# A retention layer and a multiplicative feed-forward on one core: every engine's queue in a new order, with casts, copies and sums shared anew

## The chip, the cores and the metric

The kernel runs on one core of a Trainium2 chip. The metric is the device time of one execution in microseconds (us); lower is better. Four compute engines take part: TensorE (PE, with its weight loads shown as PEld), VectorE (DVE), ScalarE (ACT) and GpSimd (POOL). SyncE (SP) issues all the DMAs, loads, stores and DMA transposes, through one queue.

## The reference

Four batches of eight heads run a linear recurrence with a decay of their own per head over 768 tokens; its output, with the heads side by side, passes through a feed-forward with two multiplied branches and two more matrices.

```python
gamma = 1.0 - 2.0 ** (-5.0 - np.arange(H))          # B, H, S, D = 4, 8, 768, 64
for t in range(S):
    state = gamma * state + k[:, :, t] (outer) v[:, :, t]
    y[:, :, t] = scale * (q[:, :, t] @ state)
x = y.transpose(0, 2, 1, 3).reshape(3072, 512)
h = (x @ w1) * (x @ w2)                              # w1, w2: 512 x 1024
out = (h @ w3) @ w_out                               # w3: 1024 x 1024, w_out: 1024 x 512
```

## The kernel before

**Tiling.** The 3072 tokens are cut into twelve chunks `n` of 256, three per batch. Matrix work is in fp16 with sums in fp32. `w3 @ w_out` is multiplied once, ahead of the tokens, into eight blocks `W3O`: `cast_w3` makes fp16 of a loaded block of w3, `turn_w3` transposes it on PE, `turned_w3` copies it out of PSUM, `w3_mm` multiplies it with a cast block of w_out, `w3_out` stores the sum in SBUF.

**A chunk.** `cast` and `cast_v` make fp16 of q, k and v; v is multiplied by a decay on the way, in `cast_v`. q and k are transposed, by PE for chunks 0 to 4 (`turn`, `turned`), and by a DMA for chunks 5 to 11 (`dma_turn`). `scores` multiplies k with q, `mask` takes the causal part out of PSUM, `kv` makes the state's increment, `state` adds it up, `inter` applies the state, `av` the masked scores. `x_out` takes x out of PSUM and multiplies it by the decay of q (table `YS` or `YN`).

**The feed-forward.** Chunks 0 and 1 multiply `W1` and `W2` in the plain way, one block of rows at a time as the weights arrive (`rows`, `rows_out`). From chunk 2 on, the two products are made by seven block products in place of eight: `combine` makes sums of weight blocks once (`WT`), `sums` makes sums of x blocks per chunk, `prod(n, u, i)` is one product (eight matmuls of 128 columns) for half `u` of the columns, `seed` and `keep_part` copy running sums out of PSUM, `c12` and `c22` add them, `half_h` multiplies the two branches. `o_unit` multiplies by `W3O`, `o_copy` scales the result into SBUF, `o_store` and `o_store_all` send it to HBM.

**Order.** Nothing is scheduled by a program: each engine executes its instructions in the order of the calls. In this text stage `n` is what stands between `inter(n, 0)` and `inter(n+1, 0)`. For n = 3 to 11 the order is a loop, whose PE part is: `inter(n,0)`, `kv(n+1)` and `scores(n+1)`, `inter(n,1)`, `av(n)`, two `o_unit(n-1, .)`, and fourteen `prod(n, ., .)`. SP too is one queue: a `dma_turn` that waits for its `cast` holds up the loads behind it. Loads go into 18 buffers (`NSTAGE`) of one pool `st`; the four `WT` tiles, and the output tiles of chunks 5 to 11, take buffers of the same pool. `fetch` is a load in the part before the loop.

Of the kernel before, what the change touches and what calls it, by code (L numbers as in the profile page):

```python
# [21 lines left out]
def kernel(  # L22
# [16 lines left out]
    NSTAGE = 18  # L39
# [138 lines left out]
    VN = const.tile([128, 2, H], FP, name="VN")  # L178
    YS = const.tile([128, 2, NP, 128], FP, name="YS")
# [10 lines left out]
    W3O = [wpool.tile([128, DM], HP, name=f"w3o_{i}") for i in range(8)]  # L190
# [179 lines left out]
    def scores(n, tags, hp=None):  # L370
# [10 lines left out]
        else:  # L381
            ps = [bank(t, [128, NP, 2, 64]) for t in tags]
            for a in range(NP):
                for s in range(2):
                    for r, g in QUARTERS:
                        nc.tensor.matmul(
                            ps[r][half(g), a, s, :], lhsT=kT[n][half(r), s, a, half(g)],
                            rhs=qchunk(n, r, a, s, g), start=True, stop=True,
# [144 lines left out]
    def x_out(n, g):  # L533
# [5 lines left out]
        if n < EO:  # L539
# [4 lines left out]
            )  # L544
        else:
# [73 lines left out]
    def o_unit(n, tb, tags, cuts=((0, 512),)):  # L619
        assert ht_n[n] == 4  # L620
        for (c0, c1), tag in zip(cuts, tags):
# [3 lines left out]
            for f in range(8):  # L625
                for x in range(parts):
                    nc.tensor.matmul(  # L627
                        ps[:, x * w : (x + 1) * w], lhsT=HT[n][:, tb, f, :], rhs=W3O[f][:, c0 + x * w : c0 + (x + 1) * w],
# [4 lines left out]
    def o_part(n, tb, x, tag):  # L633
# [4 lines left out]
        for f in range(4 * x, 4 * x + 4):  # L638
            nc.tensor.matmul(  # L639
                ps[:, :], lhsT=HT[n][:, tb, f, :], rhs=W3O[f][:, :], start=(f == 0), stop=(f == 7),  # L640
            )
# [15 lines left out]
    def o_copy(n, tb, c0=0, c1=512):  # L657
        nc.scalar.activation(o_tile(n, tb)[:, c0:c1], o_ps.pop((n, tb, c0, c1))[:, :], AF.Copy, scale=final_scale)  # L658
        o_n[n] = o_n.get(n, 0) + (c1 - c0)
        o_n[n, tb] = o_n.get((n, tb), 0) + (c1 - c0)  # L660

# [170 lines left out]
    fetch("r1")  # L832
    fetch("r5")
    fetch("r4")
    fetch("wo0")
    fetch("r2")
    fetch("wo2")
    fetch("r3")
    fetch("wo1")
    fetch("r6")  # L840
    fetch("k0")
    fetch("r7")
    fetch("wo3")
# [12 lines left out]
    fetch("w20")
    fetch("w23")
    fetch("k2")
    fetch("q2")
    fetch("q4")  # L860
    fetch("v2")
    fetch("q3")
    fetch("k3")
    fetch("v3")
    late_numbers()
    cast_w3_half(1, 0, "g")
    cast_w3_half(1, 1, "v")
    numbers()
    identity()
    keeps()  # L870
    cast_w3_half(4, 1, "g")
    cast_w3(2, "g")
    warm(2, "F2")
    warm(8, "X1")
    warm(3, "F2")
    turn_w3_half(1, 0, "F0")
    warm(3, "F2")
    turn_w3_half(1, 1, "S0")
    turn_w3_half(4, 1, "S0")
# [72 lines left out]
    w3_out(6, "s")
    cast_w3(0, "g")
    step_decays()
    w3_out(3, "v")
    mask(0, 0, 0)
    mask(0, 1, 0)
    state(0, 1)
    mask(0, 0, 1)
    w3_out(7, "s")  # L960
    state(0, 2)
    mask(0, 1, 1)
    inter(0, 0, ("F0", "X1"))
    turn("q", 1, "F1")
    turn_w3(0, "S0")
    fence(0)
    state(0, 3)
    turned_w3(0, "v")
    inter(0, 1)
    av(0)  # L970
    cast("k", 1, "s")
    turned("q", 1, "v")
    cast_wh(W1, "w1", 1, 0, "s")
    turn("k", 1, "X0")
    cast_v(1, "g")
    turned("k", 1, "v")
    x_out(0, 0)
    x_out(0, 1)
    w3_mm(0, 0)
    w3_mm(0, 2)  # L980
    scores(1, ("S0", "X0"), 1)
    w3_mm(0, 3)
    cast_wh(W1, "w1", 1, 1, "g")
    mask(1, 1, 1)
    w3_mm(0, 1)
    scores(1, ("F0", "K"), 0)
    kv(1, ("S1", "X1"))
    rows(W1, 0, 0, 1)
    cast_wc(W1, "w1", 0, 0, "g")
    cast_wh(W1, "w1", 3, 0, "g")  # L990
    cast_wc(W1, "w1", 2, 1, "g")
    cast_wc(W1, "w1", 2, 0, "g")
    w3_out(0, "s")
    cast_wc(W1, "w1", 0, 1, "s")
    cast_wh(W1, "w1", 3, 1, "s")
    mask(1, 1, 0)
    mask(1, 0, 1)
    state(1, 1)
    rows(W1, 0, 0, 0)
    rows(W1, 0, 1, 0)  # L1000
    rows(W1, 0, 1, 1)
    inter(1, 0, ("S0", "S1"))
    rows(W1, 0, 1, 3)
    rows(W1, 0, 0, 3)
    rows(W1, 0, 1, 2)
    fence(1)
    mask(1, 0, 0)
    state(1, 2)
    rows_out("a", 0, 1, 0, "s")
    cast_wh(W2, "w2", 1, 0, "v")  # L1010
    cast_wh(W2, "w2", 1, 1, "v")
    cast_wc(W2, "w2", 2, 1, "g")
    inter(1, 1)
    av(1)
    rows(W1, 0, 0, 2)
    rows_out("a", 0, 1, 1, "v")
    rows_out("a", 0, 0, 1, "s")
    cast_wc(W2, "w2", 2, 0, "s")
    cast_wh(W2, "w2", 3, 1, "s")
    x_out(1, 0)  # L1020
    rows(W2, 0, 1, 2)
    rows(W2, 0, 1, 1)
    rows(W2, 0, 0, 1)
    rows_out("a", 0, 0, 0, "v")
# [36 lines left out]
    rows(W2, 1, 0, 3)
    rows(W2, 1, 0, 0)
    rows(W2, 1, 1, 2)
    rows(W2, 1, 1, 0)
    rows(W2, 1, 1, 3)
    rows(W2, 1, 1, 1)
    o_part(0, 1, 0, "F0")
    turn("q", 2, "S0")
    turn("k", 2, "F2")
    turned("k", 2, "s")  # L1070
    turned("q", 2, "s")
    o_part(0, 0, 0, "F1")
    o_part(0, 0, 1, "X0")
    o_part(0, 1, 1, "S1")
    o_copy(0, 0)
    o_copy(0, 1)
    cast("k", 3, "s")
    rows_out("b", 1, 0, 1)
    rows_out("b", 1, 1, 1)
    rows_out("b", 1, 0, 0)  # L1080
    combine(2, 1)
    rows_out("b", 1, 1, 0)
    combine(2, 0)
    combine(4, 0)
    combine(4, 1)
    scores(2, ("S1", "F2"), 0)
    scores(2, ("S0", "X0"), 1)
    kv(2, ("K", "X1"))
    mask(2, 1, 0)
    state(2, 1)  # L1090
    mask(2, 1, 1)
    mask(2, 0, 0)
    mask(2, 0, 1)
    o_unit(1, 0, ("F1",))
    turn("k", 3, "F0")
    inter(2, 0, ("X1", "X0"))
    fence(2)
    kv(3, ("K", "F2"))
    inter(2, 1)
    av(2)  # L1100
    o_copy(1, 0)
    turned("k", 3, "s")
    state(3, 1)
    cast("q", 3, "g")
    turn("q", 3, "S1")
    o_unit(1, 1, ("S0",))
    fetch("v4")
# [160 lines left out]
```

## Time and profile before

| | |
|---|---|
| time, median of 3 runs | 176.74 us (176.43 to 178.31) |
| profiled execution: span from first to last instruction | 175.2 us |
| PE busy, share of the span | 167.0 us, 95% |
| DVE, POOL, ACT busy | 123.8, 95.0, 88.4 us (71, 54, 50%) |
| SP's DMA queue, time of its packets as a share of 16 engines | 93.6% |
| HBM read, written | 29.36 MB, 6.29 MB |
| granted TensorE clock | 1.0 throughout |

The span leaves out what lies ahead of the first instruction and behind the last one; the median of the runs is 1.5 us above it. The page does not give the profiled execution a time of its own beside the span. Matmuls are pipelined, so that a PE that is shown as busy may still be waiting between two matmuls; the start times of the matmuls tell more than the busy share.

### The profile page before, as it was taken

What the parts mean: (1) busy time and instruction counts of PE and PEld (TensorE: products, weight loads), DVE (VectorE), ACT (ScalarE), POOL (GpSimd) and SP (SyncE); (2) the same over time, 40 slices, a digit from 0 to 9 for tenths busy, and PEclk for the clock granted to TensorE, in tenths of its full rate; (3) what the DMA queues carried; (4) which work ended last, traced back from release to release, by engine and by line L of the source; (5) the groups of instructions that cost most, each with busy time, mean ns of one, the idle gap of its engine ahead of it and who ended that gap; (6) DMA issues with size and microseconds to landing.
All of it is one profiled execution on the core that took longest, in us unless ns stands there. A gap on an engine that the chain in (4) does not pass through costs nothing.

```text
span 175.2 us, 7306 instructions
## 1 busy us (share of the span) xinstructions
PE 167.0 (95%) x3196; PEld 135.9 (78%) x3196; DVE 123.8 (71%) x230; ACT 88.4 (50%) x160; POOL 95.0 (54%) x124
## 2 busy tenths in 40 slices
PE   7769999999999998999999999999999999999993
PEld 2349987878877698498799986959999598695972
DVE  0454168989899758777968689686796868956370
ACT  2025986534426884182561835618357183471832
POOL 3872267866054826079584792957819366123150
PEclk9999999999999999999999999999999999999999
DMA  5999999999999989998999999999991354092563
GB/s 206 396 418 361 314 324 344 410 391 292 282 218 218 248 187 241 146 221 182 181 241 184 163 235 165 229 183 187 195 179 24 64 201 167 9 397 80 237 247 121
DMA packets 76160, 39.80 MB, mean 227 GB/s; under 512 B 53088, under 2 KB 71776, under 8 KB 76128
## 3 DMA queue, kind: packets, MB, share of 16 engines
q1 hardware_dynamic: 76128, 39.33, 93.6%
q8 instruction: 25, 0.41, 1.0%
q14 instruction: 7, 0.06, 0.1%
HBM read 29.36 MB, written 6.29 MB: 204 GB/s over the span
## 4 chain that ended last, share of the span: by engine, by line
PE 74%; DMA 11%; SPq 9%; POOL 2%; ACT 1%; issue 1%; ACTq 0%
PE psF L752 24%; PE psF L627 9%; PE psX L627 8%; PE psK L752 5%; PE psS L627 5%; DMA st<-in_v_dram 5%; PE psX L752 5%; SPq L98 5%; SPq L85 4%; DMA st<-in_q_dram 3%; PE psF L604 3%; DMA st<-in_moe_w_dram 3%; PE psX L499 2%; PE psS L604 2%; PE psF L639 2%; PE psX L525 2%
## 5 line engine op out<-in xcount | busy, mean ns | idle before, releaser
L752 PEld LDWEIGHTS <-wt 128*128 128x128 f16 x640 | 37.4, 98 | 0.0
L627 PEld LDWEIGHTS <-ht 128*128 128x128 f16 x224 | 20.8, 98 | 14.6
L65 POOL TENSOR_TENSOR c<-u,p 128x512 f32<-128x512 f32 x20 | 25.1, 1277 | 10.9 <-DVE ht L65 9.0
L752 PEld LDWEIGHTS <-w 128*128 128x128 f16 x480 | 28.9, 98 | 2.1 <-issue 0.3
L62 ACT COPY u<-psF 128x512 f32<-128x512 f32 x40 | 23.4, 591 | 7.4 <-PE psF L752 7.3
L65 POOL TENSOR_TENSOR seven<-xt,seven 128x256 f16<-128x256 f16 x9 | 6.0, 672 | 33.5 <-PE psF L752 26.3
L65 POOL TENSOR_TENSOR v<-st,VN 128x1024 f16<-128x1024 f32 x9 | 17.2, 1907 | 4.4 <-PE psX L377 4.4
L752 PE MATMUL psF<-sodd,wt 128*128 128x128 f16 x240 | 18.1, 219 | 0.0
L65 DVE TENSOR_TENSOR c<-psK,u 128x512 f32<-128x512 f32 x10 | 6.9, 691 | 15.4 <-PE psK L752 13.7
L627 PE MATMUL psF<-w3o,ht 128*128 128x256 f16 (+1 forms) x96 | 17.2, 327 | 0.0
L546 DVE TENSOR_TENSOR xt<-psX,YN 128x512 f16<-128x512 f32 x18 | 11.6, 686 | 6.2 <-PE psX L525 6.2
L65 DVE TENSOR_TENSOR ht<-psF,c 128x512 f16<-128x512 f32 x20 | 13.7, 687 | 2.5 <-POOL c L65 2.1
L658 ACT ACTIVATE osb<-psF 128x512 f32<-128x512 f32 x8 | 4.8, 597 | 20.9 <-PE psF L627 18.3
L627 PE MATMUL psX<-w3o,ht 128*128 128x512 f16 (+1 forms) x80 | 15.2, 336 | 0.0
L65 DVE TENSOR_TENSOR ht<-psX,c 128x512 f16<-128x512 f32 x19 | 13.1, 691 | 1.9
L62 POOL CAST k<-st 128x1024 f16<-128x1024 f32 x9 | 9.4, 1046 | 8.2 <-DMA st<-in_k_dram 8.2
L604 PEld LDWEIGHTS <-w 128*128 128x128 f16 x128 | 12.1, 98 | 2.2 <-POOL w L62 0.4
L276 PEld LDWEIGHTS <-w3t 128*128 128x128 f16 x128 | 12.0, 98 | 1.4
L752 PE MATMUL psX<-xt,w 128*128 128x128 f16 x152 | 11.6, 219 | 0.0
L403 DVE TENSOR_TENSOR am<-psS,keep 128x512 f16<-128x512 f32 x17 | 10.9, 681 | 0.0
L752 PE MATMUL psF<-xt,w 128*128 128x128 f16 x160 | 10.6, 219 | 0.0
L752 PE MATMUL psF<-seven,wt 128*128 128x128 f16 x160 | 10.6, 219 | 0.0
(151 smaller groups left out, 353.7 us busy)
## 6 DMA issues: line engine op xcount, KB each, us to landing
st<-in_moe_w_dram SPq DMA_DIRECT2D x16, 512.0 KB, 7.7
st<-in_q_dram SPq DMA_DIRECT2D x12, 512.0 KB, 6.6
st<-in_k_dram SPq DMA_DIRECT2D x18, 256.0 KB, 5.2
st<-in_v_dram SPq DMA_DIRECT2D x18, 256.0 KB, 4.9
out_dram<-osb SPq DMA_DIRECT2D x9, 512.0 KB, 4.9
st<-in_moe_w_out_dram SPq DMA_DIRECT2D x4, 512.0 KB, 7.7
st<-in_k_dram SPq DMA_DIRECT2D x3, 512.0 KB, 10.9
st<-in_v_dram SPq DMA_DIRECT2D x3, 512.0 KB, 8.0
```

The source lines that it names most:

```text
L62: {"v": nc.vector.tensor_copy, "g": nc.gpsimd.tensor_copy, "s": nc.scalar.copy}[eng](dst, src)
L65: (nc.vector if eng == "v" else nc.gpsimd).tensor_tensor(dst, a, b, op)
L85: via.dma_start(t[:, :].rearrange("p (h x) -> p h x", x=2 * D), src.rearrange("h (p t) d -> p h (t d)", t=2))
L98: nc.sync.dma_start(t[:, :], src[i * 128 : (i + 1) * 128, :])
L276: nc.tensor.matmul(acc[f][:, cols], lhsT=w3t[f][:, g * 128 : (g + 1) * 128], rhs=WO[i][:, r, cols], start=(first and (r, c) == (0, 0)), st ...
L403: nc.vector.tensor_tensor(t[:, :, :, :].rearrange("p a s i -> p (a s) i"), ps[:, :, :, :].rearrange("p a s i -> p (a s) i"), keep64[:, :]. ...
L499: nc.tensor.matmul(dst, lhsT=TS[n, c][half(r), a, :], rhs=rhs, start=((g, o) not in begun), stop=False, skip_group_check=True,)
L546: nc.vector.tensor_tensor(XT[n][:, :, :, :].rearrange("p t a (s x) -> p (a s) t x", s=2)[:, :, :, g * 32 : (g + 1) * 32], x[:, :, :].rearr ...
L604: nc.tensor.matmul(rows_ps[w, n, uh][j // 2][:, j % 2, :], lhsT=W[d][:, f * 128 : (f + 1) * 128], rhs=XT[n][:, :, d, :], start=(first and ...
L627: nc.tensor.matmul(ps[:, x * w : (x + 1) * w], lhsT=HT[n][:, tb, f, :], rhs=W3O[f][:, c0 + x * w : c0 + (x + 1) * w], start=(f == 0 and x ...
L658: nc.scalar.activation(o_tile(n, tb)[:, c0:c1], o_ps.pop((n, tb, c0, c1))[:, :], AF.Copy, scale=final_scale)
L752: nc.tensor.matmul(ps[:, j, :], lhsT=lhsT, rhs=rhs, start=(opens and j == 0 and c == 0), stop=(i in (2, 3, 4) and j == 3 and c == 1), skip ...
```

## The change

Every matmul, product and DMA of the kernel before is still made. What differs:

- The loop and the list before it become one flat list of calls, about 870 in both, in a new order on every engine. Loads stand between the work in place of blocks ahead of it. `identity` and `numbers` come first on POOL.
- Some casts, copies and sums are given to another engine: `keep_part(.., "p5")` and some `c22`, `state(.., 5)` and casts go to DVE, casts of weights and PSUM copies move between ACT and DVE, `sums` are shared between DVE and POOL.
- For chunks from `PRE` = 6 on, the decay of q is multiplied into q in `cast` (table `QS`), and `x_out` becomes a plain copy on ACT.
- `NSTAGE` goes from 18 to 16. `W3O` becomes one tile. `scores` sets the start flag only on the first matmuls of a bank.
- Stores begin at stage 5 in place of stage 9.
- Functions for a seven-product form of the last matrix product are added and not called.

```diff
-    NSTAGE = 18
+    NSTAGE = 16
+    PRE = 6
+        nc.scalar.activation(QS[:, :, :], vs_x[:, :, :], AF.Exp, scale=-1.0)
...
-        if nm == "q" or n < EO:
+        if nm == "q" and n >= PRE:
+            tt(
+                eng, t[:, :, :].rearrange("p t (h d) -> p h t d", d=D),
+                src[:, :].rearrange("p (h t d) -> p h t d", t=2, d=D),
+                QS[:, :, :].rearrange("p t h -> p h t").unsqueeze(3).broadcast_to((128, H, 2, D)), MULT,
+            )
+        elif nm == "q" or n < EO:
...
-                            rhs=qchunk(n, r, a, s, g), start=True, stop=True,
+                            rhs=qchunk(n, r, a, s, g), start=(a == 0 and s == 0), stop=True, skip_group_check=True,
...
+        elif n >= PRE:
+            nc.scalar.copy(
+                XT[n][:, :, :, :].rearrange("p t a (s x) -> p (a s) t x", s=2)[:, :, :, g * 32 : (g + 1) * 32],
+                x[:, :, :].rearrange("p a (s t i) -> p (a s) t i", s=2, t=2),
+            )
...
-    fetch("r1")
-    fetch("r5")
-    fetch("r4")
-    fetch("wo0")
...
-    late_numbers()
-    cast_w3_half(1, 0, "g")
-    cast_w3_half(1, 1, "v")
-    numbers()
-    identity()
...
+    fetch('r4')
+    identity()
+    warm(2, 'F2')
+    fetch('r2')
+    numbers()
+    fetch('r5')
...
+    cast_w3_half(4, 0, 'v')
+    cast_w3_half(4, 1, 'g')
...
+    cast_wo(3, 'v')
+    turn_w3_half(1, 0, 'F0')
+    turned_w3(2, 'v')
+    w3_mm(5, 3)
...
+    cast_wh(W1, 'w1', 3, 1, 's')
+    cast_wh(W1, 'w1', 3, 0, 'v')
+    scores(1, ('F0', 'K'), 0)
...
+    rows(W1, 0, 1, 3)
...
@@ stage 3 @@
+    load('q', 7)
+    inter(3, 1)
+    av(3)
...
+    dma_turn('q', 5)
+    state(4, 1)
+    cast('k', 5, 's')
...
+    dma_turn('k', 5)
+    o_unit(2, 1, ('X1',))
...
@@ stage 4 @@
+    dma_turn('k', 6)
...
+    dma_turn('q', 6)
+    cast('q', 7, 'g')
+    half_h(3, 1, 1)
+    cast('k', 8, 's')
...
@@ stage 5 @@
+    inter(5, 1)
+    av(5)
+    state(6, 1)
+    dma_turn('k', 8)
+    o_unit(4, 0, ('F1',))
+    x_out(5, 0)
+    x_out(5, 1)
+    half_h(4, 1, 1)
+    sums(5, 3, 'g')
+    o_unit(4, 1, ('X1',))
+    dma_turn('q', 7)
+    o_copy(4, 0)
+    state(6, 2)
+    sums(5, 2, 'g')
+    state(6, 3)
+    sums(5, 1)
+    cast_v(8, 'g')
+    mask(6, 1)
+    prod(5, 0, 1, 'F1')
+    state(6, 4)
+    o_copy(4, 1)
+    prod(5, 1, 1, 'F0')
+    cast('k', 7, 'v')
+    seed(5, 0, 'X0')
+    prod(5, 0, 5, 'K')
+    state(6, 5, 'v')
+    seed(5, 1, 'X1')
+    dma_turn('k', 7)
+    cast('q', 8, 'g')
...
@@ stage 6 @@
+    inter(6, 0, ('X0', 'X1'))
+    kv(7, ('K', 'F2'), (0,))
+    kv(7, ('K', 'F2'), (1,))
+    fence(6)
+    scores(7, ('S0', 'S1'))
...
```

In the new list the order of the DMAs on SP is, after the eight loads of `w1` and `w2` (26 loads, the same 26 as before): q2 k2 v2 v3 q3 k3 q4 k4 v4 q5 q6 v5 k5 k6 v6 q7, turn q5, turn k5, k8 v7 k7, turn k6, turn q6, v8 q8 k10 k9, turn k8, turn q7, turn k7, v11 q10, store 2, turn k9, turn q8, store 4, q9, and so on. The old list has, behind the same 26 loads: k2 q2 q4 v2 q3 k3 v3 v4 k4 q6 k5 v5 q5 k6, turn k5, turn q5, v6 k7 q7, turn k6, v7, turn q6, k8 q8, turn k7, v8, turn q7, k9 q9, turn k8, v9, turn q8, and so on. In the old list turn k7 stands behind k8 and q8, and turn q7 behind v8.

More of the change, by code (lines that the diff above doesn't have):

```diff
@@ L956 @@
[L956 to L968, printed above, removed]
+    fetch('r4')
[4 more added lines that the diff above has]
+    fetch('r5')
+    warm(3, 'F2')
+    fetch('r1')
+    arguments()
+    fetch('wo3')
+    tables()
+    warm(8, 'X1')
+    fetch('wo1')
+    cast_w3_half(4, 0, 'v')
@@ L969 @@
+    turn_w3(0, 'S0')
+    mask(0, 1, 1)
+    kv(0, ('F0', 'K'))
+    turned_w3(0, 's')
+    turn('k', 1, 'X0')
+    state(0, 1)
+    fetch('w10')
+    state(0, 2)
+    inter(0, 0, ('F0', 'X1'))
+    cast('q', 1, 'g')
+    fence(0)
+    w3_out(7, 'v')
+    late_tables()
     inter(0, 1)
     av(0)
[L971 to L976, printed above, removed]
+    state(0, 3)
+    w3_mm(0, 2)
+    x_out(0, 1)
@@ L977 @@
+    turn('q', 1, 'F1')
+    fetch('w21')
     x_out(0, 0)
-    x_out(0, 1)
+    cast_v(1, 'g')
+    w3_mm(0, 3)
+    turned('q', 1, 's')
     w3_mm(0, 0)
[L980 to L983, printed above, removed]
-    mask(1, 1, 1)
[L985 to L992, printed above, removed]
@@ L998 @@
+    rows(W1, 0, 0, 2)
     state(1, 1)
[L999 to L1004, printed above, removed]
+    fetch('q2')
+    inter(1, 0, ('S0', 'S1'))
+    mask(1, 0, 0)
+    cast_wh(W1, 'w1', 1, 0, 'g')
     rows(W1, 0, 1, 2)
     fence(1)
[L1007 to L1012, printed above, removed]
+    cast_wh(W1, 'w1', 1, 1, 'v')
@@ L1076 @@
-    o_copy(0, 1)
[L1077 to L1091, printed above, removed]
-    mask(2, 0, 0)
[L1093 to L1096, printed above, removed]
+    fetch('k2')
@@ new lines @@
+    load('k', 7)
+    c22(3, 0)
+    prod(3, 1, 7)
+    prod(3, 1, 2)
+    half_h(3, 0, 0)
+    keep_part(3, 1, 'u3')
+    prod(3, 0, 4)
+    half_h(3, 1, 0)
+    cast_v(6, 'g')
+    prod(3, 1, 4)
+    half_h(3, 0, 1)
+    inter(4, 0, ('X0', 'X1'))
+    kv(5, ('K', 'F2'), (0,))
+    kv(5, ('K', 'F2'), (1,))
+    scores(5, ('S0', 'S1'))
+    fence(4)
+    inter(4, 1)
+    av(4)
+    dma_turn('k', 6)
+    o_unit(3, 0, ('F1',))
+    c22(3, 1)
+    x_out(4, 1)
+    state(5, 1)
+    dma_turn('q', 6)
@@ new lines @@
+    cast('k', 9, 'g')
+    x_out(6, 1)
+    x_out(6, 0)
+    dma_turn('k', 9)
+    dma_turn('q', 8)
+    half_h(5, 1, 1)
+    o_unit(5, 1, ('X1',))
+    o_copy(5, 0)
+    o_store_all(4)
+    state(7, 2)
+    load('q', 9)
+    sums(6, 1)
+    state(7, 3)
+    sums(6, 3)
+    mask(7, 1)
+    prod(6, 0, 1, 'F1')
+    sums(6, 2, 'g')
+    o_copy(5, 1)
+    o_store(1, 0)
+    prod(6, 1, 1, 'F0')
+    state(7, 4)
+    cast('k', 10, 'g')
+    seed(6, 0, 'X0')
+    sums(6, 4)
+    prod(6, 0, 5, 'K')
+    seed(6, 1, 'X1')
@@ new lines @@
+    prod(6, 1, 4)
+    c22(6, 1)
+    half_h(6, 0, 1)
+    inter(7, 0, ('X0', 'X1'))
+    scores(8, ('S0', 'S1'))
+    fence(7)
+    kv(8, ('K', 'F2'), (0,))
+    kv(8, ('K', 'F2'), (1,))
+    inter(7, 1)
+    av(7)
+    o_unit(6, 0, ('F1',))
+    x_out(7, 1)
+    o_store_all(5)
+    cast('q', 9, 'g')
+    state(8, 1)
+    half_h(6, 1, 1)
+    dma_turn('q', 9)
+    x_out(7, 0)
+    o_unit(6, 1, ('X1',))
+    o_copy(6, 0)
+    load('q', 11)
+    state(8, 2)
+    sums(7, 3)
+    sums(7, 2)
+    load('v', 10)
@@ new lines @@
+    prod(7, 1, 4)
+    x_out(8, 1)
+    o_unit(7, 0, ('F1',))
+    c22(7, 1, 'v')
+    dma_turn('q', 10)
+    state(9, 1)
+    half_h(7, 1, 1)
+    o_unit(7, 1, ('X1',))
+    x_out(8, 0)
+    dma_turn('k', 10)
+    o_copy(7, 0)
+    cast_v(10, 'g')
+    state(9, 2)
+    sums(8, 3)
+    state(9, 3)
+    sums(8, 1)
+    prod(8, 0, 1, 'F1')
+    state(9, 4)
+    mask(9, 0)
+    prod(8, 0, 5, 'K')
+    sums(8, 2, 'g')
+    seed(8, 0, 'X0')
+    prod(8, 1, 1, 'F0')
+    mask(9, 1)
+    keep_part(8, 0, 'p5')
@@ new lines @@
+    prod(8, 1, 2)
+    c22(8, 0)
+    keep_part(8, 1, 'u3')
+    prod(8, 0, 4)
+    half_h(8, 1, 0)
+    prod(8, 1, 4)
+    c22(8, 1)
+    state(9, 5, 'v')
+    inter(9, 0, ('X0', 'X1'))
+    kv(10, ('K', 'F2'), (0,))
+    half_h(8, 0, 1)
+    kv(10, ('K', 'F2'), (1,))
+    fence(9)
+    scores(10, ('S0', 'S1'))
+    inter(9, 1)
+    av(9)
+    mask(10, 1)
+    o_unit(8, 0, ('F1',))
+    x_out(9, 1)
+    state(10, 1)
+    half_h(8, 1, 1)
+    o_unit(8, 1, ('X1',))
+    state(10, 2)
+    o_copy(8, 0)
@@ new lines @@
+    o_unit(9, 0, ('F1',))
+    x_out(10, 1)
+    state(11, 1)
+    x_out(10, 0)
+    half_h(9, 1, 1)
+    o_unit(9, 1, ('X1',))
+    o_copy(9, 0)
+    sums(10, 3)
+    mask(11, 0)
+    sums(10, 1)
+    state(11, 2)
+    prod(10, 1, 1, 'F0')
+    sums(10, 2)
+    o_copy(9, 1)
+    state(11, 3)
+    prod(10, 1, 5, 'F2')
+    seed(10, 1, 'X1')
+    mask(11, 1)
+    o_store_all(9)
+    prod(10, 0, 1, 'F1')
+    sums(10, 4)
+    prod(10, 0, 5, 'K')
+    keep_part(10, 1, 'p5', 'v')
+    seed(10, 0, 'X0')
```

987 lines of the change are left out of this document (684 added, 303 removed).

## The prediction

> **What bounds the kernel now.** I read the page first: engine shares, the forty slices, the DMA queue.
>
> ```profile
> span 175.2 us, 7306 instructions
> ...
> PE 167.0 (95%) x3196; PEld 135.9 (78%) x3196; DVE 123.8 (71%) x230; ACT 88.4 (50%) x160; POOL 95.0 (54%) x124
> ...
> PE   7769999999999998999999999999999999999993
> ...
> DMA  5999999999999989998999999999991354092563
> GB/s 206 396 418 361 314 324 344 410 391 292 282 218 218 248 187 241 146 221 182 181 241 184 163 235 165 229 183 187 195 179 24 64 201 167 9 397 80 237 247 121
> ```
>
> Two things are full: PE after the first three slices, and the DMA engines in nearly every slice until slice 29, about 130 us. The page's GB/s also gives prices: a load of 512 KB takes 1.3 us where rows are long (weights, about 400 GB/s), 1.64 us at the 320 GB/s of slices 4 to 6 (q always, k and v of chunks 0 to 2), and 2.4 us at the 218 GB/s of slices 11 and 12 (k and v of chunks 3 on).
>
> Is PE really working when it is busy? PE's timeline says so, by the starts.
>
> ```profile
> 10.66 0.40 PE L245 MATMUL psS<-ident,w3h 128*128 128x128 f16 x4 [1.68 <-POOL w3h L62]
> ...
> 12.88 1.04 PE L276 MATMUL psF<-wo,w3t 128*128 128x256 f16 x8
> ...
> 34.08 0.38 PE L604 MATMUL psF<-xt,w 128*128 128x256 f16 x2
> ...
> 63.27 0.61 PE L752 MATMUL psK<-seven,w 128*128 128x128 f16 x8 [0.23 <-ACT p L62]
> ...
> 70.37 0.28 PE L499 MATMUL psX<-qT,t 64*64 64x64 f16 x11 [0.80 <-ACT fence L510]
> ...
> 91.78 0.32 PE L499 MATMUL psX<-qT,t 64*64 64x64 f16 x16
> ...
> 93.00 1.92 PE L627 MATMUL psF<-w3o,ht 128*128 128x256 f16 x16
> ...
> 103.10 0.47 PE L386 MATMUL psS<-qT,kT 64*64 64x64 f16 x30
> ```
>
> The last idle time before the steady part is the 1.68 us ahead of 10.66. After 70.37 no gap is named any more; stage 5 begins at 91.78 and stage 6 some 11 us later. Whatever the new order does, the same matmuls remain, so it can gain only what PE loses: the start, and the 0.80 + 0.23 us near 63 to 70 (both wait for ACT, which sat on `cast('q',5,'s')` until q5 landed). And it loses whatever new wait it puts on PE.
>
> **The start.** Which load arrives when is read from the casts that waited for a DMA:
>
> ```profile
> 4.29 0.43 DVE L62 CAST w3h<-st 128x512 f16<-128x512 f32 x1 [3.08 <-DMA st<-in_moe_w_dram]
> ...
> 8.26 0.82 DVE L62 CAST wo<-st 128x1024 f16<-128x1024 f32 x1 [0.19 <-DMA st<-in_moe_w_out_dram]
> ...
> 31.75 1.04 ACT L62 CAST w<-st 64x1024 f16<-64x1024 f32 x1 [1.23 <-DMA st<-in_moe_w_dram]
> ...
> 41.00 1.39 POOL L62 CAST w<-st 64x1024 f16<-64x1024 f32 x1 [0.24 <-DMA st<-in_moe_w_dram]
> ```
>
> The 1st load is there at 4.29, the 4th at 8.26 (1.32 us each), the 19th at 31.75, the 26th at 41.00. In the new order r4 is 1st, r5 3rd (6.9), r1 4th (8.3), wo3 5th (9.6), wo1 6th (10.9). `identity` no longer stands behind a cast, so PE transposes r4 and r5 right behind its warm-up matmuls. DVE casts r5 (0.69), copies two turned halves, casts half of r1, then wo3 from 9.6 to 10.3: the first `w3_mm(5,3)` can start near 10.4 in place of 12.88. The lead of 2.4 us does not last: the first rows of the feed-forward need the 19th load in either order (w11 before, w13 now; the 18 ahead of it are the same set). Before, they start at 34.08, 2.3 us behind its landing at 31.75, since POOL was late with half of the cast. Now ACT and DVE cast the halves at once (1.04 us): rows near 32.9. So 1.2 us of lead is left, and the remaining W1 and W2 rows come as fast as PE takes them. The two waits of 1.03 us go as well (`cast('q',5)` moves to POOL, out of ACT's queue), with 0.5 us of small delays that I count between 26 and 34: **lead up to 2.7 us** by stage 5.
>
> **The casts and copies moved.** Prices, from the groups by line:
>
> ```profile
> L65 POOL TENSOR_TENSOR c<-u,p 128x512 f32<-128x512 f32 x20 | 25.1, 1277 | 10.9 <-DVE ht L65 9.0 <-ACT u L62 1.9
> L65 POOL TENSOR_TENSOR v<-st,VN 128x1024 f16<-128x1024 f32 x9 | 17.2, 1907 | 4.4 <-PE psX L377 4.4
> L546 DVE TENSOR_TENSOR xt<-psX,YN 128x512 f16<-128x512 f32 x18 | 11.6, 686 | 6.2 <-PE psX L525 6.2
> L62 POOL CAST q<-st 128x1024 f16<-128x1024 f32 x8 | 8.3, 1042 | 3.1 <-DMA st<-in_q_dram 3.1
> ...
> L62 ACT CAST w3o<-psF 128x512 f16<-128x512 f32 x2 | 1.2, 586 | 0.9 <-PE psF L276 0.9
> ```
>
> The new `cast` of q with `QS` is not in the trace; the nearest rows are the plain cast (1.04 us) below and `cast_v` (1.91 us) above. I take 1.91, the same form, so +0.87 us on POOL for each of chunks 6 to 11. (`cast('q',6,'s')` names ACT, but `tt` sends all that is not DVE to POOL.) `x_out` on ACT costs 0.59 in place of 0.69 on DVE. By these prices a steady stage asks 5.2 to 9.0 us of POOL, 4.9 to 6.7 of ACT and 8.6 to 12.2 of DVE, against 11.05 of PE. Stage 5 is the fullest for DVE: 21 instructions, 12.2 us if each takes its whole duration, 10.4 if back-to-back ones start every 0.60 us as most of them do in DVE's timeline. I take 10.4: PE covers it. If it is 12.2, about 1 us is lost in stage 5 and in stage 3.
>
> A rule speaks against such moves: the Trainium skill (GPSIMD Engine Reference, Key points) says that GpSimd shares its SBUF interfaces with VectorE and contends with VectorE instructions that have two SBUF inputs. The trace agrees:
>
> ```profile
> L65 DVE TENSOR_TENSOR wt<-w,w 128x1024 f16<-128x1024 f16 x4 | 3.4, 894 | 0.0
> ...
> L65 DVE TENSOR_TENSOR wt<-w,wt 128x1024 f16<-128x1024 f16 x4 | 2.7, 686 | 0.0
> ```
>
> The first group ran beside POOL's casts, the second did not: 0.21 us each. By this rule the `c22` and `state(.., 5)` given to DVE, two or three a stage, cost some 0.5 us more a stage on DVE, which the 10.4 us above still takes.
>
> **The DMA order: the term that decides.** SP's timeline has one long row of transfers:
>
> ```profile
> 66.92 2.83 SPq L333 DMA_TRANSPOSE kT<-k  x1
> 70.17 1.23 SPq L333 DMA_TRANSPOSE qT<-q  x1
> ...
> 93.33 3.26 SPq L333 DMA_TRANSPOSE qT<-q  x1
> ...
> 103.69 3.45 SPq L333 DMA_TRANSPOSE qT<-q  x1
> ...
> 125.88 3.15 SPq L333 DMA_TRANSPOSE qT<-q  x1
> ...
> kT<-k SPq DMA_TRANSPOSE x7, 6.6
> qT<-q SPq DMA_TRANSPOSE x7, 4.8
> ```
>
> From 93.33 (turn q7) to 125.88 (turn q10) three stages of k, v, q and two turns take 10.85 us each, and PE takes 11.05: DMA is a hair's breadth from being the bound, and a lead on PE cannot be kept where DMA has none. With 2.4 + 2.4 + 1.64 for the loads, a turn on its own costs (10.85 − 6.44)/2 = 2.2 us.
>
> The place to look is `scores(7)` in stage 6, at 103.10 before. It needs turns q7 and k7, and the new list puts turn k7 last: behind v6, q7, four turns, k8 v7 k7, v8 q8 k10 k9, turn k8 and turn q7. From 41.00 that is 9 loads of 1.64, 14 of 2.4 and 7 turns: 41.0 + 14.8 + 33.6 = 89.4, plus the turns. At 2.2 each they land at **104.8**. But they now stand in groups of 2, 2 and 3, and a turn directly behind another cost less: turn k5 was issued at 66.92, turn q5 at 70.17, and
>
> ```profile
> DMA to landing us min/median/max: 6.5/6.5/6.5
> ...
> DMA to landing us min/median/max: 4.1/4.1/4.1
> ```
>
> (of those two): landed at 73.4 and 74.3, 0.9 us apart. With 3 × 2.2 + 4 × 0.9 the last lands at **99.6**. A second bound from the other side: turn k7 waits for `cast('k',7,'v')`, which stands in DVE's queue behind eight instructions of stage 5 that follow `av(5)`. Stage 5 begins at 91.78 − 2.7 = 89.1, `av(5)` ends 1.2 us later (91.78 to 93.00), then x_out twice, half_h, three `state`, a sum and a mask, 4.0 us, and the cast, 0.7: issued at 95.0, and landing 5 to 6.6 us later: 100 to 101.6. I take 101.0, between the two and nearer to the grouped turns. Needed: 103.10 − 2.7 = 100.4. PE stands for 0.6 us, behind it nothing but the rest of the stage: **+0.6**.
>
> By the Trainium skill (DMA: Bandwidth & Descriptors, Latency and other measured facts) a DMA transpose moves 261 GB/s, an estimate of 1.0 us for 256 KB; the sum would then have no stall here. The trace has 2.2 us for a turn between loads, so this stays a rival.
>
> Other hand-offs of turns: k5 and q5 are needed 0.5 us into stage 4 (near 77.9 with the lead) and land near 77; k6 and q6 are needed at 88.9 and land near 87.5. The five 512 KB-equivalents of stores that move ahead of turn k10 (1.3 us each) are paid for by two more groups of turns. ACT's `cast('k',8,'s')` stands ahead of `o_copy(3,0)`, which frees the bank of `prod(4,0,1)`: k8 lands near 79.5, the bank is needed at 82.5. I put **+0.2** for all of these.
>
> The tail is the same: last `o_unit` in two cuts, copy, store; `o_store_all(10)` moves to 3 us before the last matmul, and 512 KB take 1.3.
>
> **Sum.** 175.2 − 2.7 + 0.6 + 0.2 = 173.3 for the span. The median of the runs stands 1.5 above the span of the profiled execution, so the forecast is **174.8**. A measurement of this kernel tells about 1% (1.8 us) from no change.
>
> **Rivals.**
>
> *The turns cost what they cost alone* (slower). Turn k7 lands at 104.8 or, with 2.6 us for k and v (a fifth more than the page's best stretch leaves when waits are counted in), 107.6. Then stage 6 starts its scores 1.7 to 4.5 us later than before, whatever PE gained until then, and no later stage gives that back. It decides from 103.10 on: 178.4 to 181, middle 179. For it: the 10.85 us per stage, and stores come on top. Against: the pair at 66.92. Chance 0.28.
>
> *Turns cheap, no stall anywhere*: −2.7 alone, or −3.3 with the whole 1.2 + 1.03 + 1.1 of the start: 173.4 to 174. For it: 10.85 includes waits of SP for buffers and casts. Chance 0.15.
>
> *The lead is eaten by small waits* (same). DVE at 12.2 us in stages 3 and 5 (+2.2), or one of the in-order queues blocked by a tile not yet landed, or rows waiting between 34 and 48 for evacuations: net −1.3 to +1.3, 176.5. It is also the case in which the change does nothing, since PE's work is the same. Chance 0.27.
>
> **How the numbers follow.** The forecast's own case, 174.2 to 175.3, has 0.30. Faster by over 1% (under 175.0): most of it and the cheap turns, 0.40. Slower by over 1%: 0.30, the solo turns and a little of the third. Between: 0.30. The range goes from 173.2, the whole lead without a stall, to 179.3, past the middle of the slow case; cases of both signs are in it, and the likeliest one's own range is 174.2 to 175.3.
>
> **What would show it.** First `w3_mm` near 10.4; first rows near 32.9; `inter(5,0)` near 89; PE's first named gap after 70 us ahead of the scores of stage 6, released by the DMA of kT, below 1.5 us; turns landing 0.9 us behind one another within a group; ten stages of 11.05 us otherwise. Wrong would be: rows not earlier than 34, a gap ahead of stage 6 of over 3 us, stages 7 to 10 longer than 11.2, or DVE busy without a break in stage 5 with `half_h` as what PE waits for.

## The result: 3.7% slower, and the profile after

The changed kernel takes 183.85 us (median of 4 runs, 182.25 to 184.96) against 176.75; the ratio is 1.0369, 95% interval 1.0293 to 1.0446. The forecast was 174.8 with a range from 173.2 to 179.3. Each ratio, here and below, is to executions of the kernel before on the same chip, and leaves out on both sides those in a slower state, over 1.5% above the fastest of their kernel, which leaves only three of ten for the kernel with one part of the change alone. The profiled execution took 183.56 us, its span is 181.9 us, 6.7 more than before. Its page:

```profile
span 181.9 us, 7285 instructions
...
PE 169.6 (93%) x3196; PEld 137.7 (76%) x3196; DVE 141.9 (78%) x249; ACT 89.1 (49%) x159; POOL 90.5 (50%) x107
...
PE   7799999999989999999699599989999999999993
...
PEclk9999999999999999999999969999999999999999
```

PE now has two holes, in slices 19 and 22 (some 86 and 100 us), and the granted clock dips in slice 23. DVE is busy 18 us more, for 19 instructions more. PE's timeline (start, duration, what, and in brackets the idle time ahead and what ended it):

```profile
10.91 0.61 PE L280 MATMUL psF<-wo,w3t 128*128 128x256 f16 x4 [0.21 <-DVE wo L63]
...
33.87 0.38 PE L619 MATMUL psK<-xt,w 128*128 128x256 f16 x2 [0.36 <-DVE am L407]
...
68.45 0.28 PE L509 MATMUL psX<-qT,t 64*64 64x64 f16 x10
...
80.46 0.33 PE L509 MATMUL psX<-qT,t 64*64 64x64 f16 x16
...
88.27 0.61 PE L867 MATMUL psK<-sodd,wt 128*128 128x128 f16 x8 [1.68 <-DVE t L66]
93.27 0.35 PE L509 MATMUL psX<-qT,t 64*64 64x64 f16 x16
...
102.94 0.61 PE L867 MATMUL psK<-seven,w 128*128 128x128 f16 x8 [2.05 <-DVE seven L66]
108.23 0.28 PE L509 MATMUL psX<-qT,t 64*64 64x64 f16 x10
...
108.62 0.49 PE L396 MATMUL psS<-qT,kT 64*64 64x64 f16 x32
...
119.31 0.32 PE L509 MATMUL psX<-qT,t 64*64 64x64 f16 x16
```

L509 at 80.46, 93.27, 108.23 and 119.31 opens stages 4 to 7. Stage 4 takes 12.8 us, stage 5 takes 15.0, stage 6 again 11.1: with 11.1 us each before, 5.6 of the 6.7 us are lost in two stages, behind two waits for DVE. What was DVE doing? Its timeline, with POOL's beside it:

```profile
49.37 1.90 POOL L66 TENSOR_TENSOR v<-st,VN 128x1024 f16<-128x1024 f32 x1
49.93 1.89 DVE L66 TENSOR_TENSOR wt<-w,w 128x1024 f16<-128x1024 f16 x1
...
85.51 1.90 POOL L66 TENSOR_TENSOR v<-st,VN 128x1024 f16<-128x1024 f32 x1
85.58 1.98 DVE L66 TENSOR_TENSOR seven<-xt,sodd 128x256 f16<-128x256 f16 x1
...
87.59 0.29 DVE L66 TENSOR_TENSOR seven<-xt,seven 128x256 f16<-128x256 f16 x1
87.80 0.42 DVE L66 TENSOR_TENSOR t<-psK,t 128x256 f16<-128x256 f32 x1
...
97.52 1.95 POOL L66 TENSOR_TENSOR v<-st,VN 128x1024 f16<-128x1024 f32 x1
98.56 1.46 DVE L63 CAST k<-st 128x1024 f16<-128x1024 f32 x1
99.43 2.38 POOL L66 TENSOR_TENSOR q<-st,QS 128x1024 f16<-128x1024 f32 x1
99.94 2.15 DVE L66 TENSOR_TENSOR t<-s,GS 128x256 f16<-128x256 f32 x1
...
102.61 0.27 DVE L66 TENSOR_TENSOR seven<-xt,seven 128x256 f16<-128x256 f16 x1
```

`sums(4,2)` at 85.58 took 1.98 us, the same form at 87.59 only 0.29. It ended at 87.56, and POOL's multiply, begun 0.07 us before it, at 87.41. `state(6,5)` at 99.94 took 2.15 us in place of 0.42 and ended 0.28 us behind POOL's cast of q8. It is not that both run slower: a VectorE instruction that reads two SBUF operands stands until POOL's instruction is over. The Trainium skill (SBUF — State Buffer, SBUF: two separate sides) calls the port pair of the two "an exclusive lock, not a bandwidth split"; the trace agrees, 1.98 us against 0.29.

Not only two-input instructions stand. DVE's cast of k7 at 98.56, with one SBUF operand, took 1.46 us beside POOL's multiply of v8, which ended at 99.47; in the run below where that multiply is replaced by fills it took 0.74. And POOL's cast of q8, behind it, took 2.38 us in place of some 1.93. By these rows DVE was late by an estimate of 0.7 us from that cast and 1.7 us from `state(6,5)` when PE came to wait 2.05 us for `sums(5,4)`.

Over the whole kernel, the groups of such instructions (count, busy us, mean ns), before and then after:

```profile
L65 DVE TENSOR_TENSOR sodd<-xt 128x256 f16<-128x256 f16 x20 | 5.6, 290 | 0.0
```

```profile
L66 DVE TENSOR_TENSOR sodd<-xt 128x256 f16<-128x256 f16 x15 | 7.6, 507 | 1.6 <-ACT xt L556 1.5
...
L66 DVE TENSOR_TENSOR t<-s,GS 128x256 f16<-128x256 f32 x5 | 3.8, 763 | 0.0
```

Why not before? There `sums(n,4)` and `state(n+1,5)` were POOL's, and stood in its queue ahead of the casts of v and q. They wait for DVE's sums, so the long casts could not begin before those were over: two small instructions served as a gate. In stages 3 to 8 the change gave DVE `sums(n,4)` and, in four of them, `state(n+1,5)`.

The clock, by windows (length, then PE, PEld, DVE, ACT, POOL busy, granted clock, DMA share, GB/s): behind the wait of 2.05 us PE ran at half speed for 3.4 us, some 1.7 us lost. The kernel before had 1.00 throughout.

```profile
104.00:107.40 3.40, 3.40 (x36) 3.40 (x34) 2.19 (x5) 1.17 (x2) 1.58 (x2) 0.51 0.99 206
```

There is a second fault, which PE's timeline hides. Turn k7, by SP's timeline and its time to landing:

```profile
99.88 1.24 SPq L343 DMA_TRANSPOSE qT<-q  x1
101.21 2.04 SPq L343 DMA_TRANSPOSE kT<-k  x1
...
122.32 2.43 SPq L343 DMA_TRANSPOSE qT<-q  x1
```

```profile
DMA to landing us min/median/max: 4.0/4.0/4.0
...
DMA to landing us min/median/max: 5.3/5.3/5.3
```

Turn k7 landed at 105.2 and turn q9 at 127.6. Before, PE asked for them at 103.1 and, in stage 8, at 125.09, so both are late against the old pace:

```profile
125.09 0.46 PE L386 MATMUL psS<-qT,kT 64*64 64x64 f16 x32
```

Here PE was later still, because of DVE, and no wait for a DMA is named. Which of the two faults sets the time, the trace alone does not say.

### The profile page after: what moved, and what is told of

The parts are those of the page before. It is cut to its first block, busy times and chain, and to the rows that moved or that the text cites. A ratio compares the mean times of both kernels' runs of the same rounds, so it can differ in the third digit from the quotient of the medians.

```text
span 181.9 us, 7285 instructions
## 1 busy us (share of the span) xinstructions
PE 169.6 (93%) x3196; PEld 137.7 (76%) x3196; DVE 141.9 (78%) x249; ACT 89.1 (49%) x159; POOL 90.5 (50%) x107
## 4 chain that ended last, share of the span: by engine, by line
PE 54%; DVE 21%; DMA 8%; issue 7%; POOL 4%; SPq 3%; ACT 1%; POOLq 0%; DVEq 0%
PE psF L867 17%; PE psF L641 5%; DMA st<-in_q_dram 5%; PE psX L867 4%; PE psX L641 4%; DVE ht L66 4%; PE psK L867 4%; PE psS L641 4%; DMA st<-in_moe_w_dram 3%; SPq L99 3%; PE psF L619 2%; DVE t L66 2%; POOL c L66 2%; DVE seven L66 2%; PE psF L280 2%
## 5 line engine op out<-in xcount | busy, mean ns | idle before, releaser
L867 PEld LDWEIGHTS <-wt 128*128 128x128 f16 x640 | 38.7, 99 | 2.7 <-issue 2.3
L867 PEld LDWEIGHTS <-w 128*128 128x128 f16 x480 | 29.8, 100 | 3.7 <-issue 2.2
L63 ACT COPY u<-psF 128x512 f32<-128x512 f32 x37 | 21.3, 588 | 14.9 <-PE psF L867 14.9
L66 POOL TENSOR_TENSOR c<-u,p 128x512 f32<-128x512 f32 x13 | 16.6, 1289 | 21.7 <-ACT u L63 17.2
L66 DVE TENSOR_TENSOR ht<-psX,c 128x512 f16<-128x512 f32 x19 | 12.8, 689 | 2.2 <-PE psX L867 1.2
L874 ACT COPY psX<-psF 128x512 f32<-128x512 f32 x19 | 10.7, 576 | 7.1 <-PE psF L867 4.5
L619 PEld LDWEIGHTS <-w 128*128 128x128 f16 x128 | 12.3, 98 | 2.0 <-issue 0.2
L867 PE MATMUL psX<-xt,w 128*128 128x128 f16 x152 | 12.5, 229 | 0.0
L66 POOL TENSOR_TENSOR q<-st,QS 128x1024 f16<-128x1024 f32 x6 | 12.1, 2013 | 0.0
L867 PE MATMUL psF<-xt,wt 128*128 128x128 f16 x160 | 11.4, 221 | 0.0
L63 POOL CAST q<-st 128x1024 f16<-128x1024 f32 x5 | 6.1, 1221 | 9.5 <-DMA st<-in_q_dram 9.4
L556 ACT CAST xt<-psX 128x512 f16<-128x512 f32 x12 | 6.5, 588 | 6.0 <-PE psX L535 6.0
```

The lines of the kernel that those rows point to most:

```text
L63: {"v": nc.vector.tensor_copy, "g": nc.gpsimd.tensor_copy, "s": nc.scalar.copy}[eng](dst, src)
L66: (nc.vector if eng == "v" else nc.gpsimd).tensor_tensor(dst, a, b, op)
L556: nc.scalar.copy(XT[n][:, :, :, :].rearrange("p t a (s x) -> p (a s) t x", s=2)[:, :, :, g * 32 : (g + 1) * 32], x[:, :, :].rearrange("p a ...
L619: nc.tensor.matmul(rows_ps[w, n, uh][j // 2][:, j % 2, :], lhsT=W[d][:, f * 128 : (f + 1) * 128], rhs=XT[n][:, :, d, :], start=(first and ...
L867: nc.tensor.matmul(ps[:, j, :], lhsT=lhsT, rhs=rhs, start=(opens and j == 0 and c == 0), stop=(i in (2, 3, 4) and j == 3 and c == 1), skip ...
L874: nc.scalar.copy(WB[n, u, "C"][:, :, :], WB[n, u, "A"][:, :, :])
```

## The experiments

Four theories were put to runs. A: POOL's long instructions block DVE, as above. B: DVE has too many instructions. C: turn k7 is late as well, only hidden. D, formed from the first runs: A and C are two stalls over the same time, and the order of the transfers is at fault beyond k7.

**POOL as long, but not reading SBUF.** The cast of v7 becomes

```diff
-    cast_v(7, 'g')
+    hold('v', 7, 2)
```

and the same for v8 and q8. `hold` copies two columns and then fills the tile twice, so this kernel leaves out the values of three chunks.

> The changed kernel with three GpSimd instructions replaced: the multiplies that cast v7, v8 and q8 (1.90, 1.95 and 2.38 us) become a copy of two columns and two fills of the same tile, which keep GpSimd as long in the same place of its queue but read no SBUF data to speak of (the values of these three chunks are left out). Theory A, GpSimd's multiply and VectorE's two-input instruction exclude each other: sums(4,2) falls from 1.98 to about 0.3 us, state(6,5) from 2.15 to 0.42, TensorE's waits of 1.68 and 2.05 us and the slow clock behind the second (about 1.6 us) go, the span comes to about 177 to 178.5. Theory B, VectorE simply has too many instructions in stages 4 and 5: nothing changes, 183 to 184. Theory C, the turn of k7 is late as well (it landed at 105.2) and was only hidden: the 1.68 goes, but TensorE then stands some 2 us ahead of the scores of stage 6, 180 to 181.

Ratio 1.0472 (1.0356 to 1.0588), longer than any of the three theories had it. DVE and POOL in stage 4, and PE in stage 6:

```profile
85.79 0.29 DVE L66 TENSOR_TENSOR seven<-xt,sodd 128x256 f16<-128x256 f16 x1
85.94 1.97 POOL L343 MEMSET v<- 128x1024 f16 x2
86.11 0.29 DVE L66 TENSOR_TENSOR seven<-xt,seven 128x256 f16<-128x256 f16 x1
```

```profile
107.69 0.45 PE L404 MATMUL psS<-qT,kT 64*64 64x64 f16 x32 [4.20 <-DMA kT<-k]
```

The second of the two DVE sums took 0.29 us right beside 1.97 us of fills: POOL's being busy alone does not block, and what the fills lack is the reading of SBUF. Both waits for DVE went with as many instructions on DVE as before, so B is out as their cause. But the time did not fall: PE, 5 us earlier at stage 6, now stood 4.2 us for turn k7. Theory C has the place right. Its time, 180 to 181, was missed: the granted clock was 0.56 for 3.4 us behind that wait, and PE stood 2.6 us more in two waits ahead of `kv`, near 122 and 134, for which the profile names no releaser (0.5 us in the changed kernel). Why is open.

**The casts behind the sums, in stages 4 to 6**, with the whole computation:

```diff
-    cast_v(7, 'g')
...
-    sums(4, 4)
+    sums(4, 4, 'g')
+    cast_v(7, 'g')
...
-    state(6, 5, 'v')
+    state(6, 5)
+    cast('q', 8, 'g')
```

> The changed kernel with the whole computation, and another order on GpSimd in stages 4 to 6: sums(4,4), sums(5,4), sums(6,4) and state(6,5) go to GpSimd, and the casts of v7, q8 and v8 stand behind them in its queue, so that they cannot start before VectorE's two-input sums are over. Theory A (exclusion): sums(4,2) and the rest of VectorE's two-input instructions in stages 4 and 5 take their 0.28 to 0.42 us again, both waits of TensorE and the slow clock go, about 178 us. Theory B (too many instructions): VectorE is relieved of about 1 us in two stages, 182.5 to 183.5. Theory C (turn k7): about 180.5, with the wait ahead of the scores of stage 6.

Ratio 1.0238 (1.0144 to 1.0332), a median of 181.75 us: between C's 180.5 and B's 182.5, so the trace has to tell. PE's waits from 48 us on, in sum, count and longest:

```profile
PE psS L396 <- DMA kT<-k: 1.9, 1, 1.9
PE psK L867 <- DVE seven L66: 1.0, 1, 1.0
PE psK L443 <- DVE ht L66: 0.9, 1, 0.9
```

The same picture: 1.9 us for turn k7 in place of the two waits for DVE in stages 4 and 5. The two that are left lie at 54 and 137 us, outside the stages that were reordered.

**The same in stages 2 to 8.**

> As the one before, and the other overlaps taken away too: combine(3,1) behind the masks of chunk 2, the casts of k6, k11 and v10 behind sums(n,4) on GpSimd in stages 3, 7 and 8. Theory A: TensorE's 1.06 us at 52 goes as well, and 0.5 to 1 us of the later stages: 175.5 to 177, at or under the kernel before. Theory B: 181.5 to 183. Theory C: 178 to 179.5, what remains being the wait ahead of the scores of stage 6.

Ratio 1.0296 (1.0199 to 1.0394), a median of 181.90 us. That is above C's 178 to 179.5 and inside B's range; again the trace decides. DVE is no longer waited for, not at 52 us either, and what is left is C's wait for turn k7, twice as long as it was priced:

```profile
PE psS L396 <- DMA kT<-k: 4.2, 1, 4.2
PE psK L443 <- issue: 0.4, 1, 0.4
```

Turn k7 landed at 107.2 here, 2.0 us later than in the changed kernel, and the granted clock was 0.56 for 3.4 us behind the wait (107.2 to 110.6). C had neither.

**One part of the change in the kernel before:** the two instructions to DVE, and nothing else.

```diff
-        sums(n, 4, "g")
+        sums(n, 4, "v" if 3 < n < 9 else "g")
...
-            state(n + 1, 5)
+            state(n + 1, 5, "v" if 3 < n < 9 else "g")
```

> The kernel before, with one part of the change alone: in stages 4 to 8 sums(n,4) and state(n+1,5) go from GpSimd to VectorE. That adds 0.28 and 0.42 us a stage to VectorE, and takes away what held GpSimd's casts of v and q until VectorE's sums were over. Theory A: the cast of v now starts some 4 us earlier and runs beside sums(n,1) and sums(n,3), which take about 1 us or more each; if TensorE has no slack there, 0.5 to 1.5 us a stage, 179 to 184; the trace shows the stretched sums in any case. Theory B and C: VectorE is 60 to 70 per cent busy there and has room for 0.7 us, and the transfers stand where they were or earlier: 176 to 177.5.

Ratio 1.0048 (0.9981 to 1.0115). The gate is gone and DVE does stand, though PE does not notice in the profiled execution (176.75 us, the shortest of the ten):

```profile
104.71 1.90 POOL L65 TENSOR_TENSOR v<-st,VN 128x1024 f16<-128x1024 f32 x1
105.86 0.90 DVE L65 TENSOR_TENSOR sodd<-xt 128x256 f16<-128x256 f16 x1
```

DVE's sums stand shorter here than in the changed kernel, 0.9 to 1.0 us at most against 1.98, and are over about when PE, busy with two `o_unit`, comes to the products that use them. That a blocked DVE costs only where PE is just behind it is argued from these rows, not tested, and with three executions in the ratio a cost of 1% is not excluded.

**Turns q7, k7 and q8 earlier**, the rest of the change as it is:

```diff
     cast('q', 7, 'g')
+    dma_turn('q', 7)
...
     load('q', 8)
+    dma_turn('k', 7)
```

> The changed kernel with one change in the order of transfers: turn q7 stands right behind turn q6, turn k7 behind the load of q8 (its cast goes to GpSimd, behind that of v7) and so ahead of k10, k9 and turn k8; turn q8 stands behind turn k8. The overlaps of GpSimd and VectorE in stages 4 and 5 stay. Theory D, two independent stalls that end at the same place (the exclusion on the side of VectorE, turn k7 at 104 to 108 us on the side of the transfers): turn k7 now lands near 97.5, but the waits of VectorE in stages 4 and 5 are as long as before, so the time hardly falls, 181 to 183.5. Theory C alone (only turn k7 counts): 177 to 179.

Ratio 1.0397 (1.0287 to 1.0507): nothing gained, as D said, though its 181 to 183.5 was missed by a little (median 184.43). Turn k7 landed at 100.7, not 97.5, and was no longer in the way:

```profile
PE psK L867 <- DVE seven L66: 1.8, 2, 1.0
PE psS L396 <- DMA qT<-q: 1.8, 1, 1.8
PE psK L867 <- DVE t L66: 1.7, 1, 1.7
```

The wait for a turn is now for turn q9, at 130.7 in stage 8. DVE's wait in stage 5 fell from 2.05 to 0.84 us, with the cast of k7 off DVE.

**Both together.**

> Both together: the order of turns of the run above, and the order on GpSimd in which its casts of v and q stand behind VectorE's two-input sums in stages 2 to 8. Theory D: neither stall is left, the stages take 11.05 us from the third on, 175.5 to 177.5. If something else still costs time, over 179.

Ratio 1.0329 (1.0258 to 1.0400): D in this form was wrong. With turn k7 out of the way, and DVE but for 1.1 us, PE stood for turn q9 in stage 8 (the profiled execution is the longest of the six, 183.96 us, so the size of the wait is its own):

```profile
128.90 0.45 PE L396 MATMUL psS<-qT,kT 64*64 64x64 f16 x32 [2.15 <-DMA qT<-q]
```

So it is not one turn in a wrong place. Ahead of turn q9 the new list has k10, k11, v11, q10 and the stores of chunks 2, 4 and 5 and a part of 1, none of them needed by then.

**Turn k7 late in the kernel before**, behind turn k8.

> The kernel before with one transfer moved: turn k7 stands behind turn k8 in SP's queue, 12 us later; nothing else changes. It then lands near 105.5 in place of 94.3, and the scores of chunk 7 want it at 103.1. Theory D: TensorE stands 2 to 2.5 us in stage 6, with up to 1.6 us of slow clock behind it, and no later stage gives it back: 178.5 to 181. If the transfers alone cost nothing: 177.

Ratio 1.0219, interval 0.9946 to 1.0491: too wide to say. In its profile PE stands 1.2 us for turn k7, where 2 to 2.5 were expected, and 2.5 us for ACT near 72, before the moved turn comes into play. The place of the stall is as expected; its price is left open.

**The cast of q5 on POOL, in the kernel before.**

> The kernel before with the cast of q5 on GpSimd in place of ScalarE, the part of the change that was to remove the waits of 0.80 and 0.23 us near 63 to 70. Both go if ScalarE's queue was their cause: 175.5 to 176.5. If q5's landing holds up GpSimd's queue in place of ScalarE's, 177 or more.

Ratio 0.9940 (0.9900 to 0.9981), about 1 us: the part of the prediction on the waits near 63 to 70 held.

**The transfers in the order of need.** The casts stand behind the sums, the stores behind the last turn; written here as a loop, per stage, with the new lines alone:

```diff
+    sums(n, 4, 'g')
+    state(n + 1, 5, 'g')
+    cast('k', n + 3, 'g')
+    dma_turn('k', n + 3)
+    cast('q', n + 3, 'g')
+    dma_turn('q', n + 3)
+    load('v', n + 4)
+    load('k', n + 5)
+    load('q', n + 5)
```

> The changed kernel's order on TensorE, VectorE and ScalarE from the third stage on, but the transfers in the order in which they are needed, as in the kernel before: per stage v(n+4), k(n+5), q(n+5), turn k(n+3), turn q(n+3), all stores of finished chunks behind the last turn, 18 staging buffers; the casts of k and q behind VectorE's two-input sums on GpSimd, the cast of v behind c22(n,1). Theory D', the order of the transfers sets the end (each transfer ahead of a needed turn that is not needed itself makes it later, and the slack of the turns was 4.4 to 4.6 us) with the exclusion on VectorE as a second stall over the same time: both are gone here, 175.5 to 177.5, at or below the kernel before. If it is over 180, neither is the cause.

Ratio 0.9970 (0.9935 to 1.0004), span 175.0 us: the whole loss is gone, and nothing is gained. Turn k7, with its landing, is early again (88.24 + 8.2 = 96.4):

```profile
88.24 4.17 SPq L343 DMA_TRANSPOSE kT<-k  x1
```

```profile
DMA to landing us min/median/max: 8.2/8.2/8.2
```

The staging buffers went back to 18 in the same run, and three `c22` and the casts of k7 and k8 went to POOL; what these cost by themselves was not separated.

**The same with the two instructions on DVE again.**

> As the run above, but sums(n,4) and state(n+1,5) are VectorE's again, so that nothing holds the casts of k and q back until VectorE's sums are over. Theory D': the transfers are early enough, and what is left is the exclusion alone: VectorE's sums and state(n+1,5) stretch to 1 to 2 us in some stages; where TensorE has no slack 1 to 1.7 us in each of two or three stages, 177.5 to 181. If the exclusion costs nothing by itself: as the run above.

Ratio 1.0274 (1.0179 to 1.0369): A by itself, with no turn late and nothing else changed against the run above. All waits are for DVE now; the one of 1.80 us:

```profile
86.34 1.97 POOL L66 TENSOR_TENSOR q<-st,QS 128x1024 f16<-128x1024 f32 x1
86.55 1.90 DVE L66 TENSOR_TENSOR seven<-xt,seven 128x256 f16<-128x256 f16 x1
...
88.38 0.41 DVE L66 TENSOR_TENSOR t<-psK,t 128x256 f16<-128x256 f32 x1
...
88.85 0.61 PE L867 MATMUL psK<-sodd,wt 128*128 128x128 f16 x8 [1.80 <-DVE t L66]
```

**Stores early, in the kernel before.**

```diff
+        if n == 5:
+            for m in (2, 3, 4):
+                o_store_all(m)
...
+        if n == 6:
+            o_store_all(5)
```

> The kernel before with one thing moved: the stores of chunks 0 to 4 (3.25 MB less one half, 6.5 us of transfers at 1.3 us per 512 KB) stand at the end of stage 5's transfers and that of chunk 5 at the end of stage 6's, ahead of the loads and turns of the stages 6 to 9, in place of behind all turns. Theory D': turns k9 and q9 land 6.5 us later than at 116.2 and about 120.5, so q9 comes some 2 us after its use at 125.1, and q10 some 3 us: 178.5 to 181, with slow clock behind a wait of over 2 us. If the transfers have more room than the profile shows: 176.5 to 177.5.

Ratio 1.0176 (1.0090 to 1.0262): C by itself, in the old order on every engine. PE stands for turn q9 and turn q10, about as worked out from 1.3 us per 512 KB against a slack of 4.4 to 4.6. Not all of the 1.8% is theirs: the wait for ACT near 71, well ahead of the moved stores, is 1.49 us in this execution and 0.80 in that of the kernel before.

```profile
128.26 0.44 PE L386 MATMUL psS<-qT,kT 64*64 64x64 f16 x32 [1.79 <-DMA qT<-q]
...
140.76 0.45 PE L386 MATMUL psS<-qT,kT 64*64 64x64 f16 x32 [0.93 <-DMA qT<-q]
```

**The decay of q and `x_out` put back.** `PRE` = 12 in the run with the order of need.

> As the run with the transfers in the order of need and the casts behind the sums, and one more part of the change undone: the casts of q6 to q11 are plain copies again (about 1.05 in place of 1.95 us on GpSimd), and x_out of chunks 6 to 11 multiplies on VectorE again (0.69 us each) in place of the copy on ScalarE (0.59). If GpSimd's 0.9 us a chunk or the shorter VectorE queue decide anything here, the stages 6 to 11 change by 0.2 us or more each, 1 us or more in sum, to either side; if TensorE covers them, as the prediction priced it, the ratio to the kernel before stays within 0.5 per cent of the 0.997 of that run: 175.5 to 177.5 against 176.5 to 177 of the kernel before.

Ratio 1.0001 (0.9962 to 1.0039), within 0.5% of 0.997: this part of the change decides nothing here.

## Why the prediction was wrong, by its own steps

**What decides.** Two things lose time, each alone nearly as much as both together, since they cover the same stretch: DVE blocked by POOL (1.0274 with the transfers in order), the transfers as the change has them (1.0296 with the overlaps gone; their order and the 16 buffers were not parted), both 1.0369, neither 0.9970. That is why the repairs of one of them, and of parts of both, brought so little.

**The casts and copies moved: the step that failed most.** It looked at the right thing, DVE's two-input instructions beside POOL's, and took 0.21 us each from the means of two groups of four. The mean of 894 ns hid one instruction. This is DVE's answer on `wt` for 40.8 to 41.5 us of the kernel before:

```profile
L65 DVE TENSOR_TENSOR wt<-w,w x2: 693/1109/1525, 40.8 to 41.4; 128x1024 f16<-128x1024 f16 x2
```

One of the two took 0.69 us and one 1.53, beside a cast of 1.39 us. The price was not 0.21 us on each but up to POOL's whole instruction on the one that meets it, here 1.7 us. And the sum of durations, 12.2 us at most for stage 5, could not show that the order of POOL's queue decides whether they meet. The sign named for it came half true: DVE was busy without a break in stage 5 and PE waited behind it, but for a sum (`seven`) and not for `half_h`. The cast of k7, priced at 0.7 us, took 1.46.

**The DMA order: right place, wrong size.** Turn k7 was put at 101.0 between 99.6 and 104.8; it landed at 105.2. The turns in groups were sized well: the seven took 10.3 us by their landings (2.2 and 0.9 would give 10.2). The loads were not: the 9 and 14 loads that were priced at 48.4 us took 53.5, waits for buffers included; 1.64 and 2.4 came from slices 4 to 6, 11 and 12, in which no turn ran. With 53.5 in place of 48.4 the sum for turns in groups gives 104.7. So the +0.6 for turn k7 was too small: PE stood 4.2 us for it where DVE no longer held PE up. And the +0.2 for all other hand-offs left out turn q9, which was never worked out and lands 2.5 us behind its use at the old pace.

**The start.** The first `w3_mm` came at 10.91 (forecast 10.4), 2.0 us ahead of before; the first rows at 33.87 (forecast 32.9), 0.2 ahead. The load of w13 landed at 31.5, about as worked out, but its casts began at 32.4 on both engines, behind `x_out` and the copies of `kT` and `qT`, and PE waited 0.36 us more for a mask that frees the bank. With 0.8 us lost at 52 to a blocked `combine(3,1)`, 0.3 us of the forecast 2.7 were left at stage 3 (68.45 against 68.72), and 0.2 at stage 4 (80.46 against 80.68), although the wait of 0.80 us at 70 is gone.

**The rivals.** "The turns cost what they cost alone" had the sign, and its landing of 104.8 is close to the measured 105.2, but by luck: its seven turns would have taken 15.4 us and took 10.3, and the loads took the 5.1 us that the turns did not. It gave 178.4 to 181; the measured time lies above, with the blocked DVE and the slow clock behind it. That PE ran at half clock for 3.4 us behind a wait of 2.05 us was in no term. Two faults at one place were not thought of at all.

## What to carry to other kernels

Where two engines exclude each other, don't add durations: look at which instruction of the one can start beside which of the other, and keep the waits that hold them apart, even where they look like small work on the wrong engine. In a transfer queue that is nearly full, everything moved ahead of a needed transfer takes its slack, so write down for each needed one its landing and its use, to the last, not only the first. When a repair brings nothing, look at what is waited for next before giving up the theory; two stalls can hide behind one another.

## What the runs showed of the hardware

A VectorE instruction with two SBUF inputs, 0.29 us alone, stood 1.98 us beside a GpSimd multiply that read SBUF, and not at all beside GpSimd fills of 1.97 us. A VectorE cast from SBUF to SBUF stood too, 1.46 us beside such a multiply against 0.74 beside the fills. A VectorE instruction that reads PSUM and one SBUF operand kept its 0.67 us beside such a multiply (`ht` at 48.74 in the changed kernel). The granted clock fell to 0.51 for 3.4 us behind a TensorE wait of 2.05 us, and to 0.56 for 3.4 us behind waits of 4.15 and 4.20 us; it stayed at 1.00 behind six waits of 1.67 to 1.86 us in five of the runs. A DMA transpose landed 0.8 to 1.4 us behind the one ahead of it when it stood directly behind another, and 1.1 to 2.5 us when it stood behind a load (the seven turns up to turn k7 in the changed kernel).
